# Later expert weights, an earlier routing list, paced gathers and a halved first load in an attention-then-routing kernel

## The chip, the cores and the metric

The kernel runs on one core of one Trainium2 chip. The metric is device time in microseconds (us) for one execution; lower is better. Before the change the median of three timed runs is 203.11 us (202.92 to 203.23). A separate execution was taken with the hardware profiler. It took 215.99 us, and its trace spans 214.3 us, so times read from the trace are about a twentieth longer in all than those of the timed runs. All positions below ("at 59.46") are microseconds from the start of that trace.

The engines are PE (matrix products; PEld is its loading of the stationary operand), DVE (vector engine), ACT (scalar engine), POOL (GpSimd, which also issues the indirect DMAs) and SP (which issues the plain DMAs). Each works through its own queue in order.

## What is computed

Two parts, one after the other. The first is a linear attention with a polynomial sketch, the second a layer of eight experts in which a hash of the token's number picks the expert:

```python
# q, k, v: (4 batches, 4 heads, 1088 positions, 32); S1, S2: (8, 32)
def phi(x):                                  # 32 -> 64 features
    a = einsum('rd,bhsd->bhsr', S1, x); b = einsum('rd,bhsd->bhsr', S2, x)
    return einsum('bhsi,bhsj->bhsij', a, b).reshape(..., 64)
q_p, k_p = phi(q), phi(k)
kv  = einsum('bhsf,bhsd->bhfd', k_p, v);  z = sum(k_p, axis=2)
x   = einsum('bhsf,bhfd->bhsd', q_p, kv) / (einsum('bhsf,bhf->bhs', q_p, z)[..., None] + 1e-6)
x   = x.transpose(0, 2, 1, 3).reshape(4352, 128)      # one row per token

expert = token_ids * 2654435761 % 8
for e in range(8):                           # w1: (8, 128, 1024), w2: (8, 1024, 128)
    out[expert == e] = maximum(x[expert == e] @ w1[e], 0) @ w2[e]
```

## The kernel before

**Attention, batch by batch.** Each batch has 1024 "main" positions and 64 "tail" positions. PE transposes k, multiplies by S to get `ab`, DVE forms features `kp` from it, and PE sums `kv` from `kp` and `va` (v with a column of ones, so that z comes along). For q, DVE transposes first (`q_blocks`), PE multiplies by S, and `q_features` makes the features `f` and transposes them to `fT`. `kv_diagonal` copies the blocks of `kv` into a block-diagonal `m`. `x_products` multiplies `fT` by `m`; `denominators` and `x_main` divide, and SP stores the rows to `x_dram`. The stores and all loads go through SP's one queue.

```python
def parts(b, tag="q"):           # in how many pieces a batch is loaded, and its rows stored
    return 2 if b == EB and tag == "q" or b == 0 and tag != "q" else 1      # EB = 2
...
load_batch(0) ... load_batch(3)          # k, q, v of the four batches
load_experts(range(E // 2))              # experts 0..3: two 512 KB loads each
...
def kv_diagonal(b, kv):
    copies = [nc.scalar.copy] * (2 * FB * Q)                  # 16 small copies
    if b > EB:                                                # last batch only
        both = ...; nc.scalar.copy(both[:], kv); kv = both    # PSUM to SBUF first
        copies = [nc.scalar.copy] * 6 + [nc.vector.tensor_copy] * 5 + [nc.gpsimd.tensor_copy] * 5
    ...
def x_products(b, g, fT, m):             # g: first or second half of the positions
    for h0 in range(0, H, 2):
        p = ps_x.tile(...)               # PSUM pool of two banks
        ...                              # 4 products, then ACT copies p to xes
def x_main(b, g, eng):
    if g == 0: rows_of[b] = work.tile(..., name="xs", bufs=1)     # one buffer for all batches
    eng.tensor_tensor(rows_of[b] half g, xes ..., dens ..., op=OP.mult)
    if parts(b) > 1 or g == GQ - 1: nc.sync.dma_start(x_dram rows, rows_of[b] ...)
...
for b in range(EB):                      # batches 0 and 1
    kv = kv_products(b, ...)
    abk_ps = k_products(kTs, T); abq_ps = q_products(qT, T)
    ...                                  # m, ab copies, kp of the next batch
    for g in range(GQ): x_products(b, g, fTs[g], m)
    x_tail_products(b, m_tail)
    route_rows(b)                        # one-hot rows for the routing list
    if b == 0: route_tiles()
    ...
    denominators(...); x_main(b, 0..1, nc.gpsimd); x_tail(b, nc.gpsimd)
    if b == 0: load_experts(range(E // 2, E))          # experts 4..7
    fTs = [q_features(abq, 0)]
    qT = q_blocks(q_t[b + 2], T)
    ...
b, e = EB, EB + 1                        # batches 2 and 3
kv = kv_products(b, ...)
abk_ps = k_products(kTs, T); abq_ps = q_products(qT, T)
...
m = kv_diagonal(b, kv)
abk, abq = copied(abk_ps), copied(abq_ps)
m_tail = kv_tail(b, kv)
kp = k_features(abk, T, work, "")
idx = route_list()                       # 34 small products on PE: positions of all tokens
x_products(b, 0, fTs[0], m)
denominators(b, 0, HQ)
x_main(b, 0, nc.vector)
route_end(idx)                           # DVE: the lists get (to gather) and put (to scatter)
kv = kv_products(e, ...)
fT = q_features(abq, 0)
last_m = kv_diagonal(e, kv)
fetch(0)                                 # 3 gathers of 128 rows each
x_products(b, 1, fTs[1], m)
x_tail_products(b, m_tail)
m_tail = kv_tail(e, kv)
fetch(1)
fTs = [fT, q_features(abq, 1)]
...
for g in range(GQ): x_products(e, g, fTs[g], last_m)
bring(0)                                 # PE transposes the first 3 gathered tiles (L709)
...
x_main(e, 0..1, nc.gpsimd); x_tail(e, nc.gpsimd)
```

The first 18 of 36 gathered tiles take rows of batches 0, 1 and the first half of 2 only, so that they can start before the attention is over.

**Experts.** There are 16 groups of 288 gathered rows: groups 0 to 7 use experts 0 to 7, groups 8 to 15 use them again. For each group, `layer1` (L775) makes 8 products, evicted with a relu by ACT and DVE in turn (L674, L676) from a pool of four PSUM banks; `layer2` (L782) sums 8 products for the group before. Beside them run, at fixed slots (group, column): gathers (`fetch_tile`, L668), transposes of gathered rows by DMA (`turn_in`, `join_in`), of results (`turn_out`, `join_out`), and scatters of result tiles to the output (L785).

```python
def fetch_tile(i):
    ...
    gather(xg3[k][:, j], get[:, i:i + 1], NE if i < HT else N)
...
for j in range(CT):                       # CT = 3, FC = 8, GN = 288
    at(*slot(2 + 4 * j), fetch_tile, 2 * CT + j)
at(0, 3, bring, 1)
at(1, 6, bring, 2)
rest = ST - 3 * CT                        # ST = 36
for j in range(rest):
    at(*slot(FC + 6 + j * (11 * FC - 2) // rest), fetch_tile, 3 * CT + j)
for k in range(3, ST // CT):
    first = k * CT * P // GN
    at(first - 1, 0, turn_in, k); at(first - 1, 5, join_in, k)
for g in range(2, G - 1):                 # G = 16
    at(g, 1, turn_out, (g - 1) * GN // P); at(g, 5, join_out)
    for c in (5, 7): at(g, c, scatter_next)
    at(g + 1, 2, scatter_next)
    if g == G - 3: at(g, 7, nc.gpsimd.drain)
```

Of the kernel before, what the change touches and what calls it, by code (L numbers as in the profile page):

```python
# [30 lines left out]
def kernel(  # L31
# [82 lines left out]
    def parts(b, tag="q"):  # L114


        return 2 if b == EB and tag == "q" or b == 0 and tag != "q" else 1

    k_t, v_t, q_t = [], [], []

# [328 lines left out]
    def kv_diagonal(b, kv):  # L449

        m = ms[b % 2]
        kv = kv[:, :, 0:2 * DA]
        copies = [nc.scalar.copy] * (2 * FB * Q)
        if b > EB:

            both = const.tile([P, H // 2, 2 * DA], F32, name="kv_both")
            nc.scalar.copy(both[:], kv)
            kv = both
            copies = [nc.scalar.copy] * 6 + [nc.vector.tensor_copy] * 5 + [nc.gpsimd.tensor_copy] * 5
        for f in range(FB):  # L460
            for h in range(2):
                src = kv[h * R * R + f * D:h * R * R + (f + 1) * D, :, h * DA:(h + 1) * DA]
                for t in range(Q):
                    copy = copies[(f * 2 + h) * Q + t]
                    copy(m[f][t * D:(t + 1) * D, h::2, t], src)  # L465
        return m

    def kv_tail(b, kv):

        m = m_tails[b % 2]  # L470
        for h in range(2):
            r = slice(h * R * R, (h + 1) * R * R)
            nc.scalar.copy(m[r, :, h], kv[r, :, h * DA:(h + 1) * DA])  # L473
        return m

    def q_blocks(src, n):

        qT = work.tile([P, H, n, D], F32, tag=f"qT{n}", name="qT", bufs=1)
        nc.vector.transpose(qT[:].rearrange("p h t s -> p (h t s)"), src[:].rearrange("p h t d -> p (h t d)"))
        return qT  # L480
# [57 lines left out]
    def x_products(b, g, fT, m):  # L538

        for h0 in range(0, H, 2):  # L540
            p = ps_x.tile([P, 2, Q * DA], F32, tag="x", name="x_ps")
            for h in range(2):
                for fb in range(FB):
                    nc.tensor.matmul(p[:, h], fT[:, (h0 + h) * FB + fb],  # L544
                                     m[fb][:, h0 + h].rearrange("p t d -> p (t d)"),
                                     start=(fb == 0), stop=(fb == FB - 1), skip_group_check=True)
            nc.scalar.copy(xes[b % 2][:, (g * H + h0) * Q:(g * H + h0 + 2) * Q].rearrange("p (h t) d -> p h (t d)", h=2), p[:])  # L547

    def x_tail_products(b, m):
        u, t = b % 2, b // 2  # L550
        rows = slice(u * SP, (u + 1) * SP)
        p = ps_x.tile([P, H, DA], F32, tag="x", name="x_ps")
# [53 lines left out]
    nc.scalar.copy(cp[:], seq[:, :, C - 1])  # L606
    keep_busy(2)
    k_features_of(kp, abk, 0, Q)
    qT = q_blocks(q_t[0], T)
    k_features_of(kp, abk, Q, T)  # L610
    kv = kv_products(0, (kp, va), None, upto=2)
    abq = ab_tile()
# [17 lines left out]
    for b in range(EB):  # L630
        kv = kv_products(b, (kp, va), (kp_tail, va_tail), None if b else kv)
        abk_ps = k_products(kTs, T)
        abq_ps = q_products(qT, T)
        va = values(v_t[b + 1], T, work, "")
        if b == 0:
            abt_ps = q_tail_products(qT_tail)
            route_ranks(cnt)
            route_slots()
        m = kv_diagonal(b, kv)
        abk = copied(abk_ps)  # L640
        abq = copied(abq_ps)
        m_tail = kv_tail(b, kv)
        if b == 0:
            fT_tail = q_tail_features(q_tail_copied(abt_ps))
        kp = k_features(abk, T, work, "")
        for g in range(GQ):
            x_products(b, g, fTs[g], m)
        x_tail_products(b, m_tail)
        route_rows(b)
        if b == 0:  # L650
            route_tiles()
        kTs = [transposed(k_t[b + 2], g, Q) for g in range(0, T, Q)]
        if b == 0:
            route_tiles_p()
        denominators(b, 0, GQ * HQ + H)
        for g in range(GQ):
            x_main(b, g, nc.gpsimd)
        x_tail(b, nc.gpsimd)
        if b == 0:
            load_experts(range(E // 2, E))  # L660
        fTs = [q_features(abq, 0)]
        qT = q_blocks(q_t[b + 2], T)
        if b + 1 < EB:
            fTs.append(q_features(abq, 1))

# [27 lines left out]
    CT = 3  # L693
    xg3, turned_in = {}, {}

    def fetch_tile(i):
        k, j = divmod(i, CT)
        if j == 0:
            xg3[k] = rows_in.tile([P, CT, DM], F32, tag="xg3", name="xg3", bufs=3)
        gather(xg3[k][:, j], get[:, i:i + 1], NE if i < HT else N)  # L700

    def fetch(k):
        for j in range(CT):
            fetch_tile(k * CT + j)

    def bring(k):
        xp = ps_x.tile([P, CT, P], F32, tag="x", name="xp")
# [16 lines left out]

    b, e = EB, EB + 1
    kv = kv_products(b, (kp, va), (kp_tail, va_tail))
    abk_ps = k_products(kTs, T)
    abq_ps = q_products(qT, T)
    va = values(v_t[e], T, work, "")
# [1 line left out]
    m = kv_diagonal(b, kv)  # L731
    abk, abq = copied(abk_ps), copied(abq_ps)
    m_tail = kv_tail(b, kv)
    kp = k_features(abk, T, work, "")
    idx = route_list()
    x_products(b, 0, fTs[0], m)
    denominators(b, 0, HQ)
    x_main(b, 0, nc.vector)
    route_end(idx)
    kv = kv_products(e, (kp, va), (kp_tail, va_tail))  # L740
    fT = q_features(abq, 0)
    last_m = kv_diagonal(e, kv)
    fetch(0)
    x_products(b, 1, fTs[1], m)
    x_tail_products(b, m_tail)
    m_tail = kv_tail(e, kv)
    fetch(1)
    fTs = [fT, q_features(abq, 1)]
# [8 lines left out]
    for g in range(GQ):  # L757
        x_main(e, g, nc.gpsimd)
    x_tail(e, nc.gpsimd)

    feats.release()
    hots.release()
# [127 lines left out]
    def slot(n):  # L890
        return n // FC, n % FC

    for j in range(CT):
        at(*slot(2 + 4 * j), fetch_tile, 2 * CT + j)
    at(0, 3, bring, 1)
    at(1, 6, bring, 2)
    rest = ST - 3 * CT
    for j in range(rest):
        at(*slot(FC + 6 + j * (11 * FC - 2) // rest), fetch_tile, 3 * CT + j)
    for k in range(3, ST // CT):  # L900
        first = k * CT * P // GN
        at(first - 1, 0, turn_in, k)
# [1 line left out]
    for g in range(2, G - 1):  # L904
        at(g, 1, turn_out, (g - 1) * GN // P)
        at(g, 5, join_out)
        for c in (5, 7):
            at(g, c, scatter_next)
        at(g + 1, 2, scatter_next)
        if g == G - 3:  # L910

            at(g, 7, nc.gpsimd.drain)
    tables = overflow_tables()
# [146 lines left out]
```

## Time and profile before

| what | value |
|---|---|
| timed median of three | 203.11 us |
| span of the profiled execution | 214.3 us |
| first expert product (L775) starts | 72.4 us |
| last product of PE ends, about | 207.7 us |
| PE waits over the whole span | 11.5 us |
| weights of the experts | 16 loads of 512 KB |
| gathers, scatters | 36 of each, about 1.0 us of POOL each, 1.3 us from one to the next |

The views are read like this. The engine row gives busy time, share of the span and number of instructions. The slices divide the span in 40; a digit is the busy share in tenths, and the row PEclk is the granted clock of PE in tenths of full speed. A line of the timeline has start, duration, engine, line of the kernel, operation, output and inputs, and in brackets how long the engine stood idle before it and what released it. A float product of PE takes two passes, so its count in the trace is double. A window's row gives each engine's busy time and number of instructions, then the clock, the busy share of the DMA engines and their rate in GB/s.

### The profile page before, as it was taken

The page shows a single profiled execution, that of the slowest core. Times are in us where ns is not written, and L with a number is a line of the kernel's source. Part 1 is how long each engine was busy: PE and PEld are TensorE (multiplying, and loading weights), DVE is VectorE, ACT ScalarE, POOL GpSimd, SP SyncE. Part 2 cuts the span into 40 slices and gives each one's busy share as a digit, 9 for nine tenths or more (in the row PEclk, how much of TensorE's full clock was granted, in tenths as well). Part 3 has the DMA queues.
Part 4 walks back from the last instruction along what each step waited for, and adds up shares of the span by engine and source line. Part 5 has one row for each costly group of instructions (what it writes and reads, how often), then busy time and mean ns, then how long its engine had stood idle before and what let it go on. Part 6 is the DMA issues. An engine that isn't in the chain of part 4 may idle for free. (4 is left out here: it accounts for less than half of the span.)

```text
span 214.3 us, 3291 instructions
## 1 busy us (share of the span) xinstructions
PE 195.9 (91%) x1081; PEld 161.6 (75%) x1081; DVE 106.9 (50%) x256; ACT 74.4 (35%) x226; POOL 93.5 (44%) x118
## 2 busy tenths in 40 slices
PE   8989999999968999999999897899999799999670
PEld 3788998999958877777777575577777677778670
DVE  6589899995387232334423341443441753431220
ACT  6524957638151433233223130223312323222120
POOL 6003006163067475066471576537577323307441
PEclk9999999999995899999999999699999999999996
DMA  5949999999612231132415132315224043101100
GB/s 146 280 106 251 336 350 344 345 337 342 207 49 70 60 129 52 25 70 68 98 37 108 42 93 65 74 39 113 62 54 104 23 86 86 47 14 39 37 23 11
DMA packets 39649, 25.82 MB, mean 121 GB/s; under 512 B 20698, under 2 KB 36827, under 8 KB 39632
## 3 DMA queue, kind: packets, MB, share of 16 engines
q1 hardware_dynamic: 37168, 20.98, 35.2%
q0 software_dynamic: 2304, 4.59, 7.6%
q8 instruction: 9, 0.15, 0.3%
q14 instruction: 8, 0.07, 0.1%
q10 hardware_dynamic: 160, 0.04, 0.1%
HBM read 17.47 MB, written 4.59 MB: 103 GB/s over the span
## 5 line engine op out<-in xcount | busy, mean ns | idle before, releaser
L775 PE MATMUL hp<-xT,w 128*128 128x288 f32 (+2 forms) x272 | 82.9, 398 | 4.5 <-ACT hT L674 3.5
L782 PE MATMUL op<-hT,w 128*128 128x288 f32 (+1 forms) x256 | 80.4, 404 | 1.6 <-issue 1.0
L676 DVE TENSOR_SCALAR hT<-hp 128x288 f32<-128x288 f32 (+2 forms) x68 | 29.7, 439 | 72.2 <-PE hp L775 47.1
L775 PEld LDWEIGHTS hp<-xT,w 128*128 128x128 f32 x272 | 50.0, 192 | 18.4 <-issue 2.7
L785 POOL DMA_INDIRECT out_dram<-os,put x36 | 36.3, 1008 | 57.2 <-DVE os L837 27.3
L782 PEld LDWEIGHTS op<-hT,w 128*128 128x128 f32 x256 | 48.4, 192 | 14.9 <-issue 1.3
L674 ACT ACTIVATE hT<-hp 128x288 f32<-128x288 f32 (+2 forms) x68 | 27.1, 400 | 77.8 <-PE hp L775 60.5
L668 POOL DMA_INDIRECT xg<-x_rows,get x36 | 37.1, 1031 | 11.4 <-issue 10.1
L544 PE MATMUL x_ps<-m,fT 128*128 128x132 f32 x128 | 19.1, 313 | 2.1 <-DVE fT L495 1.3
L544 PEld LDWEIGHTS x_ps<-m,fT 128*128 128x128 f32 x128 | 17.9, 222 | 2.7 <-ACT m_tail L473 1.5
L573 POOL TENSOR_TENSOR xs<-xe,den 128x512 f32<-128x512 f32 x6 | 7.6, 1292 | 21.5 <-DVE den L568 14.9
L442 PE MATMUL kv<-va,kp 128*128 128x132 f32 x128 | 15.8, 278 | 0.5 <-ACT va L605 0.5
L442 PEld LDWEIGHTS kv<-va,kp 128*128 128x128 f32 x128 | 14.9, 190 | 1.0 <-issue 1.0
L816 ACT COPY half<-op 128x288 uint16<-128x288 uint16 (+1 forms) x26 | 9.0, 400 | 11.8 <-PE op L782 9.0
L465 ACT COPY m<-kv 32x66 f32<-32x66 f32 x48 | 9.9, 206 | 5.3 <-PE kv L442 4.7
L411 DVE TENSOR_TENSOR f<-ab 128x1024 f32<-128x1024 f32 x8 | 10.4, 1305 | 0.6 <-ACT ab L399 0.5
L411 DVE TENSOR_TENSOR kp<-ab 128x1024 f32<-128x1024 f32 x8 | 9.4, 1205 | 2.7 <-ACT ab L399 2.7
L495 DVE STREAM_TRANSPOSE fT<-f 128x1024 f32<-128x1024 f32 x8 | 10.0, 1245 | 0.5
L547 ACT COPY xe<-x_ps 128x264 f32<-128x264 f32 x16 | 6.0, 379 | 11.6 <-PE x_ps L544 9.1
L837 DVE COPY os<-turned 128x256 uint16<-128x256 uint16 (+1 forms) x26 | 7.7, 339 | 3.3 <-DMA turned<-half 3.3
L383 PE MATMUL ab_ps<-s_k,kT 128*128 128x128 f32 (+3 forms) x72 | 9.0, 277 | 0.2 <-ACT kT L376 0.2
L383 PEld LDWEIGHTS ab_ps<-s_k,kT 128*128 128x128 f32 (+1 forms) x72 | 8.4, 191 | 0.9 <-ACT kT L376 0.4
(155 smaller groups left out, 141.8 us busy)
## 6 DMA issues: line engine op xcount, KB each, us to landing
w<-in_moe_w_dram SPq DMA_DIRECT2D x16, 512.0 KB
q<-in_q_dram SPq DMA_DIRECT2D x3, 512.0 KB
k<-in_k_dram SPq DMA_DIRECT2D x3, 512.0 KB
v<-in_v_dram SPq DMA_DIRECT2D x3, 512.0 KB
x_rows<-xs SPq DMA_DIRECT2D x3, 512.0 KB
xg<-x_rows,get POOLq DMA_INDIRECT x36
out_dram<-os,put POOLq DMA_INDIRECT x36
k<-in_k_dram SPq DMA_DIRECT2D x2, 256.0 KB
```

Source lines behind the costliest of these rows:

```text
L383: nc.tensor.matmul(dst, stationary, s.rearrange("p t x r -> p t (x r)").unsqueeze(1).to_broadcast([s.shape[0], n, s.shape[1], 2 * R]), sta ...
L411: eng.tensor_tensor(dst, ab[:, :, 0].unsqueeze(3).to_broadcast(shape), ab[:, :, 1].unsqueeze(2).to_broadcast(shape), op=OP.mult)
L442: nc.tensor.matmul(kv[:].rearrange("p x y -> p (x y)")[:, pr * HA:(pr + 1) * HA], kp[rows, t, 2 * pr:2 * pr + 2].rearrange("p h i j -> p ( ...
L465: copy(m[f][t * D:(t + 1) * D, h::2, t], src)
L495: nc.vector.transpose(fT[:].rearrange("p k (q s) -> p k q s", q=Q), f[:].rearrange("p q h (k d) -> p (h k) q d", d=D))
L544: nc.tensor.matmul(p[:, h], fT[:, (h0 + h) * FB + fb], m[fb][:, h0 + h].rearrange("p t d -> p (t d)"), start=(fb == 0), stop=(fb == FB - 1 ...
L668: nc.gpsimd.indirect_dma_start(out=dst, out_offset=None, in_=x_dram[0:rows], in_offset=bass.IndirectOffsetOnAxis(ap=idx, axis=0), bounds_c ...
L674: nc.scalar.activation(dst, src, AF.Relu if relu else AF.Copy)
L676: return nc.vector.tensor_scalar(dst, src, 0.0, None, op0=OP.max).ins
L775: nc.tensor.matmul(hp[:, 0:hi - lo], w1[:, g % E, c * P:(c + 1) * P], x_columns(g * GN + lo, g * GN + hi), start=True, stop=True)
L782: nc.tensor.matmul(ops[g][:, 0:hi - lo], w2[:, g % E, c], hTs[g][:, c, lo:hi], start=(c == 0), stop=(c == FC - 1))
L785: st_ = nc.gpsimd.indirect_dma_start(out=out[:], out_offset=bass.IndirectOffsetOnAxis(ap=idx, axis=0), in_=src, in_offset=None, bounds_che ...
```

## The change

It has five parts. (1) The weights of experts 6 and 7 are loaded after the rows of the last batch are stored, instead of after batch 0's with 4 and 5: less traffic lies ahead of the rows in SP's queue. (2) The routing list is computed ahead of batch 2's other products, and its end ahead of batch 3's features, so that the first gathers wait for stored rows only; the copies for `m` leave POOL, and the second half of batch 2's products uses the pool of four banks. (3) The first q is loaded, transposed and its rows stored in halves. (4) The transposed q of batches 2 and 3 is made before the routing rows instead of after them. (5) In the expert stage each gather takes its indices from a small copy that DVE makes, which holds the gather until DVE's queue has come to it; gathers stand at new slots relative to the group that needs them, scatters one column later, and POOL's drain at two other groups.

```diff
-        return 2 if b == EB and tag == "q" or b == 0 and tag != "q" else 1
+        return 2 if b == 0 or b == EB and tag == "q" else 1
...
-            copies = [nc.scalar.copy] * 6 + [nc.vector.tensor_copy] * 5 + [nc.gpsimd.tensor_copy] * 5
+            copies = [nc.scalar.copy] * 8 + [nc.vector.tensor_copy] * 8
...
-    qT = q_blocks(q_t[0], T)
+    qT = work.tile([P, H, T, D], F32, tag=f"qT{T}", name="qT", bufs=1)
+    for g in range(GQ):
+        nc.vector.transpose(qT[:, :, g * Q:(g + 1) * Q].rearrange("p h t s -> p h (t s)"),
+                            q_t[0][:, :, g * Q:(g + 1) * Q].rearrange("p h t d -> p h (t d)"))
...
         x_tail_products(b, m_tail)
+        qT = q_blocks(q_t[b + 2], T)
         route_rows(b)
...
         if b == 0:
-            load_experts(range(E // 2, E))
+            load_experts(range(E // 2, E - 2))
         fTs = [q_features(abq, 0)]
-        qT = q_blocks(q_t[b + 2], T)
...
-        gather(xg3[k][:, j], get[:, i:i + 1], NE if i < HT else N)
+        gather(xg3[k][:, j], get[:, i:i + 1] if at_once else paced(get[:, i:i + 1]), NE if i < HT else N)
+
+    def paced(idx):
+        t = moe.tile([P, 1], I32, tag="idx", name="idx", bufs=4)
+        nc.vector.tensor_copy(t[:], idx)
+        return t[:]
...
     kv = kv_products(b, (kp, va), (kp_tail, va_tail))
+    idx = route_list()
     abk_ps = k_products(kTs, T)
...
     m_tail = kv_tail(b, kv)
+    route_end(idx)
     kp = k_features(abk, T, work, "")
-    idx = route_list()
     x_products(b, 0, fTs[0], m)
     denominators(b, 0, HQ)
     x_main(b, 0, nc.vector)
-    route_end(idx)
+    fetch(0)
     kv = kv_products(e, (kp, va), (kp_tail, va_tail))
     fT = q_features(abq, 0)
     last_m = kv_diagonal(e, kv)
-    fetch(0)
-    x_products(b, 1, fTs[1], m)
-    x_tail_products(b, m_tail)
+    x_products(b, 1, fTs[1], m, bank)
+    x_tail_products(b, m_tail, bank)
...
     x_tail(e, nc.gpsimd)
+    load_experts(range(E - 2, E))
...
-    for j in range(CT):
-        at(*slot(2 + 4 * j), fetch_tile, 2 * CT + j)
     at(0, 3, bring, 1)
     at(1, 6, bring, 2)
-    rest = ST - 3 * CT
-    for j in range(rest):
-        at(*slot(FC + 6 + j * (11 * FC - 2) // rest), fetch_tile, 3 * CT + j)
+    for j, n in enumerate((1, 4, 7)):
+        at(*slot(n), fetch_tile, 2 * CT + j)
+    for k in range(3, ST // CT):
+        for j in range(CT):
+            at(*slot((k * CT * P // GN - 1) * FC - 19 + 7 * j // 2), fetch_tile, k * CT + j)
...
-        for c in (5, 7):
+        for c in (6, 7):
             at(g, c, scatter_next)
-        at(g + 1, 2, scatter_next)
-        if g == G - 3:
+        at(g + 1, 3, scatter_next)
+        if g in (G - 5, G - 2):
             at(g, 7, nc.gpsimd.drain)
```

More of the change, by code (lines that the diff above doesn't have):

```diff
@@ L536, in q_tail_features, with x_bank, x_products @@
         return fT[:].rearrange("p (k q) s -> p k (q s)", q=Q)
-    def x_products(b, g, fT, m):
+    def x_bank(shape, name):
+        return ps_x.tile(shape, F32, tag="x", name=name)
+    def x_products(b, g, fT, m, psum=x_bank):
         for h0 in range(0, H, 2):
-            p = ps_x.tile([P, 2, Q * DA], F32, tag="x", name="x_ps")
+            p = psum([P, 2, Q * DA], "x_ps")
             for h in range(2):
@@ L547, in x_products, with x_tail_products @@
             nc.scalar.copy(xes[b % 2][:, (g * H + h0) * Q:(g * H + h0 + 2) * Q].rearrange("p (h t) d -> p h (t d)", h=2), p[:])
-    def x_tail_products(b, m):
+    def x_tail_products(b, m, psum=x_bank):
         u, t = b % 2, b // 2
         rows = slice(u * SP, (u + 1) * SP)
-        p = ps_x.tile([P, H, DA], F32, tag="x", name="x_ps")
+        p = psum([P, H, DA], "x_ps")
         for pr in range(H // 2):
@@ L694, with fetch_tile @@
     xg3, turned_in = {}, {}
-    def fetch_tile(i):
+    def fetch_tile(i, at_once=False):
         k, j = divmod(i, CT)
@@ L699, in fetch_tile @@
             xg3[k] = rows_in.tile([P, CT, DM], F32, tag="xg3", name="xg3", bufs=3)
-        gather(xg3[k][:, j], get[:, i:i + 1], NE if i < HT else N)
+        gather(xg3[k][:, j], get[:, i:i + 1] if at_once else paced(get[:, i:i + 1]), NE if i < HT else N)
[3 more added lines that the diff above has]
+        return t[:]
     def fetch(k):
         for j in range(CT):
-            fetch_tile(k * CT + j)
+            fetch_tile(k * CT + j, True)
     def bring(k):
```

## The prediction, made before the changed kernel ran

> **What bounds the kernel now.** I read the page's engine row and slices first, then what the tensor engine (PE) waited for, then the timeline at each gap. Part 1 and the slices of part 2:
>
> ```profile
> PE 195.9 (91%) x1081; PEld 161.6 (75%) x1081; DVE 106.9 (50%) x256; ACT 74.4 (35%) x226; POOL 93.5 (44%) x118
> ...
> PE   8989999999968999999999897899999799999670
> PEclk9999999999995899999999999699999999999996
> ```
>
> PE is the bound: 195.9 of 214.3 us, and no other engine passes 50%. Time can only come out of PE's idle slices (the digits below 9) or out of slices in which its clock is down (PEclk 5 and 6). PE's order of products and their number do not change, so I listed every PE wait: 11.5 us in all, plus 6.6 us after its last product. The windows around the worst one, columns PE, PEld, DVE, ACT, POOL busy, then clock:
>
> ```profile
> 55.00:60.00 5.00, 5.00 (x44) 4.75 (x43) 0.97 (x3) 0.72 (x3) 0.00 (x0) 1.00 0.35 127
> 60.00:65.00 5.00, 2.61 (x22) 2.14 (x20) 4.75 (x15) 2.65 (x11) 3.75 (x7) 0.92 0.15 54
> 65.00:70.00 5.00, 5.00 (x23) 5.00 (x24) 3.47 (x6) 0.76 (x2) 3.78 (x5) 0.50 0.31 101
> ```
>
> PE is full, then half idle while DVE is full, then full again at half clock. Before the gap DVE is nearly idle (0.97 of 5). The timeline there:
>
> ```profile
> 59.46 0.69 DVE L573 TENSOR_TENSOR xs<-xe,den 128x512 f32<-128x512 f32 x1 [3.13 <-DMA x_rows<-xs]
> 60.07 0.19 DVE L355 TENSOR_SCALAR tok_none<-idx_ps 128x36 f32<-128x36 f32 x1
> ...
> 61.08 1.21 DVE L411 TENSOR_TENSOR f<-ab 128x1024 f32<-128x1024 f32 x1
> 62.33 1.25 DVE L495 STREAM_TRANSPOSE fT<-f 128x1024 f32<-128x1024 f32 x1
> ...
> 63.13 1.23 POOL L668 DMA_INDIRECT xg<-x_rows,get  x1 [0.74 <-POOL m L465]
> 63.60 1.14 DVE L465 COPY m<-kv_both 32x66 f32<-32x66 f32 x5
> 63.72 0.46 PE L544 MATMUL x_ps<-m,fT 128*128 128x132 f32 x2 [1.35 <-DVE fT L495]
> ...
> 64.89 6.59 PE L544 MATMUL x_ps<-m,fT 128*128 128x132 f32 x30 [0.71 <-DVE m L465]
> ```
>
> This is the chain to learn. DVE stood 3.13 us at the scaling of batch 2's first rows, because its tile was still being stored for batch 1. Everything behind it in DVE's queue came late: routing list, features fT, copies m. PE waited for the last two. The cause lies ten microseconds back, in the queue of stores: SP issued batch 1's rows at 50.58, after sixteen weight loads (8 MB), and they were out only at 59.4. The two small PE waits that the change also touches:
>
> ```profile
> 11.77 2.00 PE L383 MATMUL abq_ps<-s_k,qT 128*128 128x128 f32 x16 [0.75 <-DVE qT L479]
> 37.34 2.00 PE L383 MATMUL abq_ps<-s_k,qT 128*128 128x128 f32 x16 [0.53 <-DVE qT L479]
> ```
>
> [...] 512 KB of rows took 8.8 us from issue to release behind the weights. [...] the feature product took 2.05 us beside GpSimd's va copy at 37.2, 1.16 us at 33.7. [...]
>
> **Weights later (experts 6 and 7 to the end of batch 3; 4 and 5 stay).** 4 of 16 loads, 2 MB, leave the queue ahead of batch 1's rows. The page shows 336 to 350 GB/s there, so 2 MB is about 6.0 us: rows out at about 53.4 instead of 59.4. The wait at L573 could start at 56.32, so it vanishes with 3 us to spare. Cost: the 2 MB now run at about 70 to 77 us beside the first gathers. Expert 6 is first used at group 6, about 118 us; no wait there.
>
> **Routing list ahead.** The 34 products (1.27 us) move before the batch's other products: no PE time, only order. The six small DVE operations (1.1 us) run at about 50.5, in the 2.09 us in which DVE waited for ab at 52.6. The first gather then needs only the stored rows. DVE's scaling ends about 57.1, the store about 59.5 (my allowance of 2 us, from the wait for an output store at the end of the trace, longest 2.1), gathers issue at 59.6 to 63.2 at 1.3 us each instead of 63.13 to 67.0.
>
> **m copies (6/5/5 to 8/8/0) and PSUM banks.** ACT takes 8 x 0.257 = 2.05 us from 59.9, DVE 8 x 0.228 = 1.8 us from 59.9, since its features ran before. m is ready at 62.0 instead of 64.7. GpSimd drops 2.37 us and can gather. The second half of batch 2's products goes to the four-bank pool, which drops the 0.34 us wait for ACT's copy. PE: kv ends 59.58, 16 passes to 61.6, tail to 62.1, then batch 3's products at once; the second half's features come at 64.2, just in time. Saved: 0.34 + 1.35 + 0.71 = **2.4 us**, about 0.1 given back.
>
> **q in halves.** PE wanted qT at 11.02 and DVE was free at 9.74, but the whole q had not landed until 10.47. With a half, DVE transposes 0.63 us from about 9.8. Saved up to 0.75; I take **0.7**. The rows of batch 0 are then also stored in two parts, off the path.
>
> **qT of the next batch before the routing rows.** Removes the 0.53 us at 37.34. DVE was busy 4.86 to 4.97 of each 5 us from 30 to 50, so what it gains it partly owes: I take **0.3**.
>
> **Paced gathers and later scatters.** 30 gathers get a one-column DVE copy. The nearest row is the 128x1 cast at 0.15 us: 4.5 us on a DVE that is under 40% busy in the expert stage and has four PSUM banks of slack. Free, unless a copy stands before an eviction that is already late. The gain is in order: gathers no longer queue behind scatters that wait for data. From 72.4 to 207.7 PE waits were 6.2 us (at 120, 135, 167 and 201). The profiled execution took 215.99 us and the timed median is 203.11, and these gaps are first among what the timed runs may not have. Take away all of the 11.5 us of waits but the early ones and the two throttled stretches (about 3.0 us at 65 to 71, 30 passes at 0.22 instead of 0.12; about 2.2 at 135 to 139) and the timed 203.11 is already nearly reached. So I credit **0** here.
>
> **Sum.** 203.11 - (2.4 - 0.1) - 0.7 - 0.3 = 199.8. The throttled 3.0 us at 65 goes too if timed runs have it; at one chance in four that is 0.75 off. New waits described below put about 0.45 back. **199.5 us**, 1.8% less.
>
> **Rivals.** First: a new wait for gathers takes the place. PE would reach the second transposed tile group at about 69.0, when its last gather (issued by 67.1) lands about 69.1; the third at 77.1, with its gathers issued by 73.7 into the moved weight traffic. For: both margins are under 2 us[...]. Against: gathers are 64 KB, and the DMA share in those windows was 0.14 to 0.41 of 5 before. Would leave 201 to 202. Second: the clock dip is in the timed runs too, and goes with the gap. For: the dip follows the gap directly in the trace; against: the sum above has no room for 3 us. Would make 196.5 to 197. Third: DVE becomes the bound from 15 to 55 us and swallows the early gains: 200.5 to 201. Fourth: pacing removes gaps in the expert stage that timed runs do have: each is 1.0 to 2.1 us, so 197 to 198.5.
>
> **Range and chances.** Center 199.5, low 196.8 (second or fourth rival), high 202.2 (first and third together). Two per cent is 199.05, just under my centre: faster 0.41, within 0.57, slower 0.02. A loss over 2% would need a wait of more than 7 us where I find margins of one or two.
>
> **What would show it.** Right: L573 on DVE without a DMA wait; first gather at about 58 to 60; first expert product at about 66 to 67 instead of 72.39; no PEclk 5 near 65; the waits at 11.77 and 37.34 gone; batch 1's rows out by 54. Wrong: PE waiting at the first transposes (L709) for gathers; an expert product waiting for weights; DVE waiting for ACT or PE so that features come late at 40 or 53; evictions late behind the index copies. If the first expert product comes 5 us earlier and the timed gain is much under 2 us, the gap was mostly the profiled execution's own, and my reading of it as timed cost fails.

## The result and the profile after

The changed kernel takes 204.93 us (median, 204.53 to 205.21) against 203.17 for the kernel before (202.92 to 203.57). The ratio is 1.0083, 95% interval 1.0057 to 1.0109. It is 0.8% slower, where 1.8% faster was predicted. The profiled execution of the changed kernel spans 203.0 us.

The engine row and the slices of the changed kernel:

```profile
PE 191.7 (94%) x1081; PEld 158.7 (78%) x1081; DVE 109.1 (54%) x290; ACT 75.0 (37%) x228; POOL 93.8 (46%) x113
...
PE   8999999999997899899999999999999999999970
PEclk9999999999999699999999999999999999999997
```

PE is still the bound. One dip of the clock is left, near 68 us, and the expert stage from 90 us on is full. The windows around the middle, with the same columns as those shown of before:

```profile
55.00:60.00 5.00, 5.00 (x43) 4.62 (x41) 4.45 (x11) 1.82 (x8) 0.00 (x0) 1.00 0.16 56
60.00:65.00 5.00, 4.55 (x38) 4.08 (x37) 3.69 (x6) 2.87 (x11) 4.21 (x3) 1.00 0.17 55
65.00:70.00 5.00, 3.44 (x11) 2.42 (x12) 0.65 (x3) 1.37 (x4) 4.09 (x5) 0.75 0.29 85
```

DVE is busy from 55 us on (4.45 of 5 instead of 0.97), as intended, and PE keeps 4.55 of the next 5 us. The idle time has moved on to 65 to 70 us, where DVE has nothing to do. The timelines of the changed kernel, of DVE, GpSimd and PE in turn:

```profile
54.86 0.69 DVE L576 TENSOR_TENSOR xs<-xe,den 128x512 f32<-128x512 f32 x1
```
```profile
60.16 2.20 POOL L674 DMA_INDIRECT xg<-x_rows,get  x1 [10.14 <-DVE m L465]
62.67 1.00 POOL L674 DMA_INDIRECT xg<-x_rows,get  x1 [0.31 <-issue]
63.98 1.00 POOL L674 DMA_INDIRECT xg<-x_rows,get  x1 [0.30 <-issue]
```
```profile
62.75 2.04 PE L547 MATMUL x_ps<-m,fT 128*128 128x132 f32 x16 [0.34 <-DVE den L570]
64.62 0.27 PE L722 MATMUL xp<-ident,xg 128*128 128x128 f32 x1
65.27 0.33 PE L722 MATMUL xp<-ident,xg 128*128 128x128 f32 x1 [0.38 <-DMA xg<-x_rows,get]
66.69 0.33 PE L722 MATMUL xp<-ident,xg 128*128 128x128 f32 x1 [1.09 <-DMA xg<-x_rows,get]
...
67.60 3.82 PE L789 MATMUL hp<-xT,w 128*128 128x288 f32 x8 [0.20 <-ACT xT L680]
...
80.31 0.38 PE L722 MATMUL xp<-ident,xg 128*128 128x128 f32 x2
81.91 0.33 PE L722 MATMUL xp<-ident,xg 128*128 128x128 f32 x1 [1.22 <-DMA xg<-x_rows,idx]
```

The scaling (L576, the old L573) no longer waits for the store. But PE now waits at the transposes for gathered rows, three times: 0.38 and 1.09 us at the first group, 1.22 us at the third. GpSimd's first gather is put down to DVE's copies of `m`, which stand behind it in the program. What it reads are the rows whose store SP issued at 55.59; it starts 4.57 us after that (in e11, below, the same wait is put down to that store). After the waits at the first group, the first eight expert passes take 3.82 us.

**The kernel before, profiled again.** The profile that the prediction read spans 214.3 us, far from the timed 203. A second profile of the same kernel (e1, below, on chip A) spans 201.8 us. Its PE timeline:

```profile
62.67 1.81 PE L544 MATMUL x_ps<-m,fT 128*128 128x132 f32 x14 [0.59 <-DVE m L465]
65.28 2.04 PE L544 MATMUL x_ps<-m,fT 128*128 128x132 f32 x16 [0.79 <-DVE den L567]
...
68.48 2.21 PE L775 MATMUL hp<-xT,w 128*128 128x288 f32 x8 [0.20 <-ACT xT L674]
...
71.58 0.33 PE L709 MATMUL xp<-ident,xg 128*128 128x128 f32 x1 [0.68 <-DMA xg<-x_rows,get]
...
80.47 0.49 PE L709 MATMUL xp<-ident,xg 128*128 128x128 f32 x3
```

The gap in the middle is there, but with no half clock behind it (1.00 from 65 to 70 us), and no wait at the third group (80.47). The first expert product starts at 68.48, not 72.39. This is the profile to compare with. From it to the changed kernel:

| term | us |
|---|---|
| first expert product, 68.48 to 67.60 | -0.88 |
| its first eight passes, 2.21 to 3.82 (half clock) | +1.61 |
| wait at the second group, 0.68 to none | -0.68 |
| wait at the third group, none to 1.22 | +1.22 |
| sum | +1.27 |
| measured: end of the last product, 195.60 to 196.74 | +1.14 |

The timed medians differ by 1.76 us. The terms are not independent: a PE that loses less to half clock reaches the third group earlier and waits there longer, as e7 shows.

### The profile page after: what moved, and what is told of

Same layout as the page of the kernel before. It is cut to its first block, busy times and chain, and to the rows that moved or that the text cites. A ratio compares the mean times of both kernels' runs of the same rounds, so it can differ in the third digit from the quotient of the medians.

```text
span 203.0 us, 3360 instructions
## 1 busy us (share of the span) xinstructions
PE 191.7 (94%) x1081; PEld 158.7 (78%) x1081; DVE 109.1 (54%) x290; ACT 75.0 (37%) x228; POOL 93.8 (46%) x113
## 5 line engine op out<-in xcount | busy, mean ns | idle before, releaser
L796 PE MATMUL op<-hT,w 128*128 128x288 f32 (+1 forms) x256 | 79.1, 399 | 0.0
L789 PEld LDWEIGHTS hp<-xT,w 128*128 128x128 f32 x272 | 50.8, 194 | 13.4 <-ACT xT L680 0.3
L796 PEld LDWEIGHTS op<-hT,w 128*128 128x128 f32 x256 | 47.7, 190 | 12.5
L674 POOL DMA_INDIRECT xg<-x_rows,idx x30 | 31.2, 1040 | 26.0 <-DVE idx L712 19.5
L547 PE MATMUL x_ps<-m,fT 128*128 128x132 f32 x128 | 16.3, 281 | 0.5 <-DVE den L570 0.3
L547 PEld LDWEIGHTS x_ps<-m,fT 128*128 128x128 f32 x128 | 15.0, 190 | 1.2 <-issue 0.5
L576 POOL TENSOR_TENSOR xs<-xe,den 128x512 f32<-128x512 f32 x6 | 7.7, 1300 | 17.2 <-DVE den L571 17.2
L674 POOL DMA_INDIRECT xg<-x_rows,get x6 | 7.2, 1200 | 11.7 <-DVE m L465 10.1
```

Of the source, the lines that this page charges most:

```text
L547: nc.tensor.matmul(p[:, h], fT[:, (h0 + h) * FB + fb], m[fb][:, h0 + h].rearrange("p t d -> p (t d)"), start=(fb == 0), stop=(fb == FB - 1 ...
L674: nc.gpsimd.indirect_dma_start(out=dst, out_offset=None, in_=x_dram[0:rows], in_offset=bass.IndirectOffsetOnAxis(ap=idx, axis=0), bounds_c ...
L789: nc.tensor.matmul(hp[:, 0:hi - lo], w1[:, g % E, c * P:(c + 1) * P], x_columns(g * GN + lo, g * GN + hi), start=True, stop=True)
L796: nc.tensor.matmul(ops[g][:, 0:hi - lo], w2[:, g % E, c], hTs[g][:, c, lo:hi], start=(c == 0), stop=(c == FC - 1))
```

## The experiments

The theory to be tested: the late place of the weights of experts 6 and 7 is what costs. Their 2 MB run beside the third group's gathers and delay them. It has three rivals, which are not the prediction's four. Rival one: the pacing (part 5) delays the gathers. Rival two: the half-clock stretch behind the wait at the first group is the whole loss. Rival three: the routing list and the copies (part 2) delay PE.

Each group of four ran on one chip with the kernel before beside it: e1 to e4 on chip A (median of before: 203.47 us), e5 to e8 on B (209.03), e9 to e12 on C (209.38), e13 to e16 on D (209.55). The changed kernel itself was run again only on C (e9). On B, C and D the profiles show short stalls in the expert stage that A's mostly do not. So ratios are compared within a chip.

The first ratio, with its interval, leaves out runs more than 1.5% above the fastest of their kernel, which takes away 3 of the 60 runs of the kernel before on A, 28 of 51 on B, 25 of 43 on C and 1 of 11 on D. The last column is the median of all runs over that of the kernel before. On B and C the two differ by up to 1.1%, because the kernel before scatters widely there; changed versions compared with one another hardly depend on the choice. No interval lies beyond 2% either way, so the differences here are all small; for e8 and e12 the comparison with before is unclear.

| kernel | ratio to before | 95% interval | median, us | over median of before |
|---|---|---|---|---|
| A: e1 before, again | 0.9996 | 0.9974 to 1.0018 | 203.28 | 0.9991 |
| A: e2 without pacing | 1.0017 | 0.9964 to 1.0070 | 204.65 | 1.0058 |
| A: e3 without routing list ahead | 1.0057 | 1.0031 to 1.0084 | 204.76 | 1.0063 |
| A: e4 without late weights | 0.9994 | 0.9972 to 1.0016 | 203.03 | 0.9978 |
| B: e5 weights after third group | 0.9996 | 0.9957 to 1.0035 | 207.24 | 0.9914 |
| B: e6 weights after batch 1 | 0.9903 | 0.9875 to 0.9930 | 205.69 | 0.9840 |
| B: e7 idle products | 1.0013 | 0.9983 to 1.0042 | 207.23 | 0.9914 |
| B: e8 e6 without pacing | 1.0114 | 1.0044 to 1.0185 | 209.30 | 1.0013 |
| C: e9 changed kernel, again | 0.9993 | 0.9956 to 1.0029 | 206.99 | 0.9886 |
| C: e10 before + weights after batch 1 | 0.9936 | 0.9866 to 1.0006 | 207.75 | 0.9922 |
| C: e11 e6 again | 0.9866 | 0.9828 to 0.9904 | 205.08 | 0.9795 |
| C: e12 e11 + idle products | 0.9880 | 0.9822 to 0.9938 | 204.83 | 0.9783 |
| D: e13 e4 again | 0.9911 | 0.9879 to 0.9944 | 207.38 | 0.9896 |
| D: e14 before + pacing | 0.9891 | 0.9843 to 0.9938 | 207.76 | 0.9915 |
| D: e15 before + pacing + weights after batch 1 | 0.9843 | 0.9806 to 0.9880 | 205.79 | 0.9821 |
| D: e16 e6 again | 0.9869 | 0.9835 to 0.9903 | 206.47 | 0.9853 |

### e1: the kernel before, unchanged

> The kernel before, unchanged, for a profile whose span fits its timed runs. Theory A (the changed kernel's PE now reaches its first transposes before their rows are gathered, idles, and its clock falls): this profile shows neither the DVE wait of 3.1 us turning into a throttled stretch at 65 us nor PE waits of 1 to 2 us in the expert stage; time 203.2 +- 0.4, first expert product 68 to 70 us. Theory B (pacing costs time by itself): same time, but the expert stage here is shorter than the changed kernel's by about 1.5 us.

Measured: 203.28 us. The profile is the one shown above. It says what part of the first profile the timed runs as a rule have: 0.33 + 0.59 + 0.79 = 1.71 us of gap in the middle, 0.53 us at the second batch's `qT`; not the half clock at 65, not the wait of 0.75 us at 11.77, not the gaps of 1.0 to 2.1 us in the expert stage.

### e2: pacing undone

```diff
-        gather(xg3[k][:, j], get[:, i:i + 1] if at_once else paced(get[:, i:i + 1]), ...)
+        gather(xg3[k][:, j], get[:, i:i + 1], ...)
# and the gather, scatter and drain slots of before
```

> The changed kernel with the pacing and the new slots taken back. Theory A: the wait at the first transposes (1.5 us) and the slow clock after it stay, only the wait at the third group of transposes (1.2 us, at 81.9) can go; 203.3 to 204.5. Theory B: the whole loss goes with the pacing; 202.5 to 203.2. Theory C (the weights moved behind the rows now run into the gathers): the wait at the third group stays nearly whole, about 204.5.

Measured: 204.65 us; the interval does not separate it from the changed kernel or from before. The first expert product starts at 66.11, and PE still waits at the third group (0.17 and 0.61 us), since the gathers land 4.8, 6.2 and 6.8 us after issue with no pacing at all. So rival one does not explain the waits. The wait at the first group and the half clock behind it, which Theory A expected to stay, are absent from this profile (2.21 us for the first eight passes, mean clock 1.00 from 68 to 90 us).

### e3: routing list, copies and banks undone

```diff
-    idx = route_list()          # ahead of k_products
+    idx = route_list()          # behind k_features, as before
-    ... [nc.scalar.copy] * 8 + [nc.vector.tensor_copy] * 8
+    ... [nc.scalar.copy] * 6 + [nc.vector.tensor_copy] * 5 + [nc.gpsimd.tensor_copy] * 5
# fetch(0), route_end and the PSUM bank likewise
```

> The changed kernel with the routing list, the first gathers, the m copies and the PSUM bank put back where they were. Theory A: PE loses about 2 us before its last attention products but then waits less for gathers, so about the same, 204 to 205.5. If part 2 is what made it slower: 202.5 to 203.2. If part 2 brought the predicted 2.4 us and something else lost 4: 206.5 to 207.5.

Measured: 204.76 us, still slower than before. The first expert product starts at 66.68, no later than in the changed kernel, and the third group's wait is 1.64 us, followed by half clock within 81 to 86 us (mean clock 0.92 from 68 to 90 us). So rival three falls, and so does what the prediction made of part 2: with the rows out early, the old order was no later.

### e4: late weights undone

```diff
-            load_experts(range(E // 2, E - 2))
+            load_experts(range(E // 2, E))
...
-    load_experts(range(E - 2, E))
```

> The changed kernel with experts 6 and 7 loaded with 4 and 5 again, before the rows. Theory C: the gathers at 72 to 77 us land in 2.7 us and the PE wait at 81.9 goes, 202.5 to 203.7. Theory A alone: the rows of batch 1 are stored later, DVE waits again, the first gather and the first expert product come 1 to 3 us later, 205 to 207.

Measured: 203.03 us, level with before, where the changed kernel was 0.8% slower on the chip of the result (it was not run on A) and e3, which keeps the late weights, 0.6% slower on A. In these comparisons this one edit takes the loss away. The landing of the third group's gathers, first of the changed kernel and then of e4 (there with one more, the last of the second group):

```profile
L674 POOL DMA_INDIRECT xg<-x_rows,idx x3: 1000/1000/1037, 71.9 to 74.6; - x3
...
DMA to landing us min/median/max: 4.4/6.6/6.7
```
```profile
DMA to landing us min/median/max: 2.5/2.6/2.7
```

The windows of the changed kernel and of e4 around them (the last column is the DMA rate in GB/s):

```profile
72.00:75.00 3.00, 3.00 (x14) 2.32 (x14) 1.47 (x6) 1.23 (x3) 2.39 (x3) 1.00 0.85 281
75.00:78.00 3.00, 3.00 (x14) 2.37 (x13) 0.98 (x3) 0.41 (x1) 2.39 (x3) 1.00 1.08 336
```
```profile
72.00:75.00 3.00, 3.00 (x14) 2.34 (x13) 1.40 (x6) 1.23 (x3) 2.31 (x3) 1.00 0.59 208
75.00:78.00 3.00, 3.00 (x14) 2.37 (x13) 1.04 (x4) 0.41 (x1) 2.09 (x4) 1.00 0.16 44
```

The gathers move 64 KB each, and the instruction on GpSimd still takes 1.0 us. What grows is the time to landing, 4 us more with the weights at 336 GB/s beside them. By what mechanism the weights hold the gathers up is not shown.

In e4 the scaling waits for the store again (2.23 us, at 57.36), and the first expert product starts at 68.36, about where e1 has it. What part 1 was for is lost, and the time is still better than with it.

### e5: weights after the third group, in program order

```diff
-    load_experts(range(E - 2, E))
...
     at(1, 6, bring, 2)
+    at(1, 7, load_experts, range(E - 2, E))
```

> The changed kernel with experts 6 and 7 loaded just after the third group of transposes (group 1, last column) instead of before it. Theory D (the late weights slow the first gathers from 2.6 to 6.6 us to landing, PE waits for them, and the wait can pull the clock down): the first expert product stays at 66 to 67.6, the gathers of the third group land in 2.6 us, no PE wait at 80 to 82, 201.0 to 202.2. Rival (any 2 MB moved into the expert stage costs it the same wherever it stands, through the transposes by DMA and later gathers): 204 to 205.

Measured: 207.24 us, 0.9996 of before. A miss that teaches: the edit moves the loads behind the transposes in the program, but the loads depend on nothing that PE does, and did not wait for it. The trace has the same traffic (283 GB/s from 72 to 76 us, 341 from 76 to 80) ahead of the third group's transposes, which start at 80.04, and the same wait there (1.29 us). It is the changed kernel once more.

### e6: weights after batch 1's rows

```diff
             load_experts(range(E // 2, E - 2))
+        else:
+            load_experts(range(E - 2, E))
...
-    load_experts(range(E - 2, E))
```

> The changed kernel with experts 6 and 7 loaded right after the rows of batch 1, where its DMA engines stand nearly idle from 50 to 56 us. Theory D: rows of batch 1 still out by 54, no weights beside the gathers, first expert product at 66 to 67.5, 201.0 to 202.2. Rival: the store of batch 2's first rows at 55.6 now waits behind the 2 MB (6 us), gathers begin 1 to 2 us later and PE waits at the first transposes; 202.5 to 204.

Measured: 205.69 us, 1% less than before and 0.7% less than e5 (205.69 / 207.24). The loads are issued at 49.5 to 51.6, behind batch 1's rows and clear of the third group's gathers. The scaling at 55.09 waits for nothing, and neither do the third transposes. The half clock is still there (0.50 from 69 to 72 us). So the early rows can be kept without the collision.

### e7: idle products ahead of the waiting transposes

```diff
+            if k in (0, 2) and j > 0:      # 2 and 4 idle 128x512 products
+                for _ in range(2 * j):
+                    nc.tensor.matmul(idle[:], ..., start=True, stop=True)
             nc.tensor.transpose(xp[:, j], xg3[k][:, j], ident[:])
```

> The changed kernel with idle products (2 and 4 of 128x512, bf16, their result unused) in front of the second and third tile of the first and the third group of transposes, where PE waits for gathers. The waits remain in length, but PE isn't idle in them. If the slow clock is part of the loss: mean clock up from 0.986 to 0.994 or more, no throttled stretch at 67 to 71 or 81 to 86, about 1.7 us less (a stretch of 3.4 us at half speed), 203.0 to 203.6. If only the waits count: 204.6 to 205.2, or a little more for the added products.

Measured: 207.23 us, no different from e5 at 207.24. The clock stays at full rate through the middle (1.00 in every microsecond from 58 to 90 us), so the idle products do what they are for, but no time is gained. The traces show two reasons. The idle products take PE themselves: the six at the first group 1.6 us (0.59 + 1.03). And a PE that comes earlier to the third group waits there longer. First e5, then e7:

```profile
80.04 0.38 PE L722 MATMUL xp<-ident,xg 128*128 128x128 f32 x2
81.71 0.33 PE L722 MATMUL xp<-ident,xg 128*128 128x128 f32 x1 [1.29 <-DMA xg<-x_rows,idx]
```
```profile
78.55 0.27 PE L726 MATMUL xp<-ident,xg 128*128 128x128 f32 x1
81.08 0.33 PE L726 MATMUL xp<-ident,xg 128*128 128x128 f32 x1 [0.51 <-DMA xg<-x_rows,idx]
```

PE arrives 1.49 us earlier in e7 and leaves 0.63 us earlier, when the last gather has landed. So rival two, that the half clock is the whole loss, is not borne out. The end of e9 to e12 shows that it is a part of it.

### e8: e6 without pacing

The edits of e6 and of e2 together.

> As the kernel with the weights after batch 1's rows, with the pacing and the new slots taken back too. Theory D says that the pacing has nothing to do with the loss: within 0.6 us of that kernel. If the order of gathers and scatters brings something, this one has a PE wait of 1 us or more near 116 and is slower by 0.7 to 1.5 us; if the copies cost, it is faster by 0.7 or more.

Measured: 209.30 us, 1.0114 of before; with pacing (e6) it was 0.9903, on the same chip. Here taking the pacing away costs about 2%, though from six runs that scatter from 206.05 to 210.63. The expectation that pacing has nothing to do with the loss (within 0.6 us of e6) was missed. The profile, of the fastest of these runs, has no wait over 0.7 us in the expert stage and does not show where the time goes. On A pacing made no clear difference: e4, which has it, is level with before. e13 to e16 come back to this.

### e9 to e12: the two kernels on one chip, and e6's edit alone

e9 is the changed kernel, e11 the kernel of e6. e10 is the kernel before with e6's place for the weights. e12 is e11 with e7's idle products at the first group only.

> The changed kernel as it is, on the same chip as the next three, so that they can be compared with it as well as with the kernel before. Every theory: 1.005 to 1.011 of the kernel before (1.0083 measured), PE waits of 1.0 to 1.3 us at the third group's transposes near 81 us and of 1 us in all or more at the first group's near 66.

> The kernel before with only the load of experts 6 and 7 moved, from behind batch 0's rows to behind batch 1's; routing list, copies, first q and gather slots as before. If the place of the load is the whole matter (the moved weights help where they bring batch 1's rows out early and hurt where they lie beside the third group's gathers): 0.99 of the kernel before or a little under, about the same as experts 6 and 7 after batch 1 in the changed kernel. If the gain of that kernel came from the pieces going together (list ahead, copies off GpSimd, slots): 0.995 to 1.005, since in the kernel before the first gathers wait for the routing list and not for the rows alone.

> The changed kernel with experts 6 and 7 loaded behind batch 1's rows, a second time, now on the chip of the changed kernel itself. If the weights beside the third gathers are the loss: 0.985 to 0.993 of the kernel before and 1.5 to 2.5 us under the changed kernel, third gathers landing in about 2.6 us and no wait at the third transposes. If the first figure was chance: within 0.5% of the changed kernel.

> The kernel of e11 with 2 and 4 idle products of 128x512 ahead of the second and third tile's transposes of the first group, the only ones that still wait. If a throttled stretch behind that wait costs what it seemed to (8 products 1.7 us late): 0.5 to 1.7 us under e11, and no slice at half clock near 68 to 72 us. If the idle products take up what they save, as when they were put into the changed kernel: within 0.5 us of e11.

Measured: 206.99, 207.75, 205.08 and 204.83 us. The windows of e9 and of e11, from the first expert products to 90 us:

```profile
68.00:90.00 22.00, 19.19 (x79) 14.41 (x79) 7.22 (x28) 5.85 (x15) 12.30 (x14) 1.00 0.52 155
```
```profile
68.00:90.00 22.00, 21.42 (x91) 16.33 (x90) 7.68 (x29) 7.06 (x18) 13.92 (x15) 1.00 0.22 65
```

Both run at full clock here, and e9 gets 12 passes less done in 22 us. PE at the third group, first of e9 and then of e11:

```profile
78.84 0.33 PE L722 MATMUL xp<-ident,xg 128*128 128x128 f32 x1 [0.66 <-DMA xg<-x_rows,idx]
80.66 0.33 PE L722 MATMUL xp<-ident,xg 128*128 128x128 f32 x1 [1.48 <-DMA xg<-x_rows,idx]
```
```profile
78.84 0.49 PE L724 MATMUL xp<-ident,xg 128*128 128x128 f32 x3
```

With the weights moved, 2.1 us of waits are gone, and the timed median falls by 1.9 us (206.99 - 205.08); the intervals to the kernel before do not touch. This is the loss in two profiles with no half clock in them. e9's first expert product starts at 65.66, e11's at 67.08: PE was ahead by 1.4 us and lost it all, and more, to the third group.

The expectation for e9 was missed: on this chip the changed kernel is level with before by the first ratio, and 1.1% below it by the medians. So the loss of 0.8% against the kernel before is not found on every chip; what holds on both B and C is the loss against the same kernel with the weights moved. e10 falls between its two readings and settles nothing by itself. e12 is within 0.25 us of e11: idle products are worth nothing here either.

**Half clock in the timed runs.** Each run has its mean granted clock on record. All seven profiled executions at 0.988 or less have a slice of the span at 8 tenths of the clock or less ahead of the last one; none of the eleven at 0.991 or more has. So the timed runs can be sorted by it (number of runs and their median in us):

| kernel | at 0.988 or less | at 0.991 or more |
|---|---|---|
| A: before | 5: 204.59 | 49: 203.43 |
| A: e3 (weights late) | 15: 205.18 | 5: 203.41 |
| A: e4 (weights early) | 8: 203.76 | 12: 202.77 |
| B: e5 (weights late) | 5: 207.60 | 6: 206.61 |
| B: e6 (after batch 1) | 11: 205.88 | 8: 204.85 |
| B: e7 (late, idle products) | none | 22: 207.23 |
| C: e9 (weights late) | 5: 207.31 | 7: 206.38 |
| C: e11 (after batch 1) | 7: 205.92 | 14: 204.44 |
| C: e12 (after batch 1, idle products) | none | 6: 204.83 |

Within one kernel the runs with half clock are 0.9 to 1.8 us longer. At like clock, moving the weights still saves 1.4 to 1.9 us on B and C. So there are two losses, and the place of the weights is one of them with or without the other. Idle products keep the clock up in every run and cost 0.4 to 0.6 us over the runs that had it up anyway, which is about what they save on average over all runs. All four runs behind the result are at 0.985 to 0.987: the loss measured there holds both. e3's five runs at high clock are level with before. The sorting is by what happened and not by an edit, so how the two share the 1.76 us of the result stays open.

### e13 to e16: what pacing is worth

e13 is e4's kernel, e16 is e6's. e14 is the kernel before with part 5 alone. e15 is the kernel before with part 5 and e6's place for the weights.

> The changed kernel with all experts 4 to 7 loaded after batch 0's rows again (as e4), beside e14 to e16 on one chip. If the harm is only in the end-of-batch-3 place of two experts: as good as e16, within 0.5% of it. If bringing batch 1's rows out early is worth something in itself: slower than e16 by 0.4% or more (first expert product near 68.4 instead of 67).

> The kernel before with the fifth part alone: gathers paced by copied indices, new slots for gathers and scatters, drain at other groups; weights, routing list, copies and first q as before. If pacing is free and idle, as the prediction credited it: 0.997 to 1.003 of the kernel before. If it takes stalls out of the expert stage of timed runs (the prediction's fourth rival): 0.98 to 0.99.

> The kernel before with two things: experts 6 and 7 loaded after batch 1's rows, and the pacing with its slots. If these two hold all of the gain of e16: within 0.4% of e16. If the routing list ahead, the copies and the q parts carry a share: slower than e16 by 0.4% or more.

> The changed kernel with experts 6 and 7 loaded after batch 1's rows, as e11, as the measure for e13 to e15 on their chip: 0.985 to 0.998 of the kernel before; nearer 0.998 if this chip shows no short stalls in the expert stage of the kernel before, nearer 0.985 if it does.

Measured: 207.38, 207.76, 205.79 and 206.47 us. Pacing alone is worth 1.1% on this chip. Together with e6's place for the weights it is worth 1.6%, the best ratio on this chip, and that kernel has neither the routing list ahead nor the copies off GpSimd nor the q parts. The expected reading "these two hold all of the gain" holds: parts 2 to 4 add nothing that was measured (six runs each). That early rows are worth something beside pacing is likely but not settled: e16 is 0.4% under e13, which meets both readings of that expectation, and e15 0.5% under e14, with intervals that overlap.

What pacing may do is looked for in the expert stage, one line each of the first profile of before, of e10 (no pacing, chip C) and of e15 (pacing, chip D):

```profile
134.95 0.72 PE L775 MATMUL hp<-xT,w 128*128 128x288 f32 x2 [2.12 <-ACT hT L674]
```
```profile
129.74 0.95 PE L777 MATMUL hp<-xT,w 128*128 128x288 f32 x2 [2.04 <-ACT half L818]
```
```profile
124.17 0.75 PE L787 MATMUL hp<-xT,w 128*128 128x288 f32 x2 [1.56 <-ACT hT L679]
```

And the window from 90 to 190 us of e10 and of e15:

```profile
90.00:190.00 100.00, 97.96 (x398) 75.99 (x397) 40.75 (x121) 26.43 (x71) 52.99 (x53) 0.98 0.30 69
```
```profile
90.00:190.00 100.00, 97.46 (x409) 76.00 (x408) 41.99 (x144) 27.61 (x75) 50.49 (x51) 1.00 0.26 67
```

The stalls are there with pacing too, and as much of them in all (2.54 us against 2.04), but no single one was over 1.6 us and no half clock followed: 409 passes against 398. In the two profiles without pacing a stall of 2 us was followed by one. These are single profiles of different chips, and the clocks of the timed runs on D do not point to half clock as the reason for the 1.1%: of the kernel before 10 of 11 runs are at 0.989 or more, of e14 two of six at 0.985. Where the 1.1% comes from, what causes the stalls, and why chip A has hardly any, stays open.

## Why the prediction was wrong

**Weights later.** The first half was right: the wait at L573 vanished, and the scaling could start at 54.86. The step that failed is its cost. The prediction saw that the 2 MB would run "beside the first gathers", but charged only "Expert 6 is first used at group 6, about 118 us; no wait there", and in the sum "about 0.45" for all new waits. That asked when the moved weights are needed, and not what they hold up. The gathers beside them landed in 6.6 us instead of 2.6, and PE waited 1.22 us (2.14 in e9). e5 against e6 and e9 against e11, each pair on one chip, show that this place of the load costs 0.7 to 0.9%; e4 agrees. The half clock (0.9 to 1.8 us where it comes) is the other part of the loss in the result; how they share it stays open.

**Routing list ahead.** The gathers' readiness was mis-sized. The list was early (its last operation at 50.55), and the scaling ended 1.5 us earlier than predicted (55.55 against 57.1), but the gather started 4.57 us after SP issued the store (4.25 in e9), for which "my allowance of 2 us" stood. The two errors nearly cancel: the gather was predicted at 59.6 and started at 60.16, in e9 at 59.37. That is luck. The first gather then took 2.20 us on GpSimd, where the prediction's trace had 1.23, and landing took 2.6 us and not 2.0. So the third tile came at 66.6 and not near 64.2 (59.6 + 2 x 1.3 + 2.0). In e9 the first gather took 1.23 us again and PE did not wait at the first group at all, so this wait is not in every execution.

**m copies and banks.** "Saved: 0.34 + 1.35 + 0.71 = 2.4 us" took its sizes from an execution 11 us longer than the timed ones. In e1 the gap is 0.33 (ACT's copy) + 0.59 (copies of m) + 0.79 (denominators) = 1.71 us, with no wait for features, and the changed kernel has 0.34 + 0.38 + 1.09 = 1.81 us in their place. The old waits were cured; the gathers' chain ended right behind them. In this stage nothing was gained.

**q in halves, qT earlier.** The sum was about right, the split was not. In PE's timelines the changed kernel is 0.2 us ahead at the first q's products (10.81 against 11.01) and 0.98 us ahead at the next batch's (35.60 against 36.58). The wait of 0.75 us that the halves were to remove was the first profile's own. So about 1.0 us was predicted and was there at 36 us. At the first expert product 0.88 us was left, with the other parts mixed in; in e4, which has the same halves, 0.12 (68.36 against 68.48). In time nothing of it was seen: e15 has neither part and is no slower than e16.

**Pacing.** The credit of 0 holds on chip A, where the expert stage is full in e1, e3 and e4, with and without pacing. On D pacing is worth 1.1%, the size of the prediction's fourth rival; that it came by that rival's way, by removing gaps, is not shown.

**The rivals.** The first was what happened, down to the groups: "its gathers issued by 73.7 into the moved weight traffic". It was sized as a gain lost, at 201 to 202, and not as a loss, for two reasons: the landing of 2 us, and the clock. The prediction counted half clock only as something that could go away. In the changed kernel it came behind a new wait: 1.61 us. The second rival was wrong: the timed kernel before mostly has no such dip to lose (5 of 60 runs on A are at a clock of 0.988 or less). The third was not seen: DVE did not end any of the waits that grew.

**The warning.** The prediction's last sentence was that a first expert product 5 us earlier with a gain much under 2 us would show the gap to be mostly the profiled execution's own. It came 4.8 us earlier (72.39 to 67.60) with no gain. So it was, for the half clock and the later start, though not for 1.71 us of waits.

## What to carry to other kernels

Before a load is moved, look at what runs on the DMA engines where it goes, not only at when its data is needed: here small gathers that the tensor engine was to use a few microseconds later took 4 us more. In e5 a load was not held back by its place between another engine's instructions (its traffic ran from 72 us, they from 80); in e6 its place in its own issuer's queue put it where it did no harm (issued at 49.5 to 51.6 us). Earlier work can be lost again at the next wait: e9 was 1.4 us ahead and e7 1.49, and the third group's gathers took it back. And where the profiled execution is much longer than the timed ones, a wait's size should be taken from a second profile before it is put into a sum.

## What the runs showed of the hardware

Half clock came after short waits, and not each time. In the changed kernel two waits of 0.38 and 1.09 us within 1.8 us were followed by it (0.50 from about 67.5 to 70.9 us, eight passes in 3.82 us), and in e6 0.29 and 1.12 us (3.30 us). Waits of 0.44 and 1.02 us in e11 and 0.43 and 0.98 us in e16 were not (2.21 us for the eight passes in both). One and the same kernel shows it both ways: with waits of 0.41 and 1.3 us before its last attention products, e4's profile stays at full clock (16 passes in 2.04 us) and e13's runs at half from about 65 us (3.71 us for the same 16); of e11's 22 timed runs 7 are at a mean clock of 0.985 or less and 14 at 0.991 or more. So the lengths of the waits alone do not tell whether half clock follows; what else decides it is not shown.
